# Chunk 4's columns on partitions without TensorE transposes

## The chip, the core and the metric

The kernel runs on one core of one Trainium2 chip. The metric is the device time of one execution in microseconds. A core has TensorE (PE, with its weight loads as PEld), VectorE (DVE), ScalarE (ACT), GpSimd (POOL) and SyncE (SP). SP does no arithmetic here; it issues most of the transfers, ACT and POOL issue the rest.

## What is computed

There are 2048 positions of 448 channels. With `xn` the layer norm of q over the channels, the result is a sum of three:

```python
xn = (q - mean) / sqrt(var + 1e-5)
ks = sum(k_pad[t:t+S] * shift_k[:, 3-t] for t in range(4))   # short causal filter
kv = ks * v
y  = causal_conv(kv, ssm_k) + kv * ssm_D                     # 2048 taps per channel, by FFT
out = q + xn * y + mish(xn @ w1 + b1) @ w2                   # w1 448x1792, w2 1792x448
```

The result is to have the accuracy of float32, so every dense product is made of three products of parts (a high part, rounded to the fast float32 form, and the low remainder).

## The kernel before

The positions are cut into 8 chunks of 256 (two halves `jj` of 128 each), and the 1792 hidden features into 7 pairs of 128. The program is a row of *slots*, two for each chunk and pair. An even slot holds the first dense layer of pair i (`g1_mm`, 22 matmuls, L509). An odd slot holds Mish of pair i (`mish`, L517, then the split into `ach` on ScalarE, L81, and `acl` on VectorE, L82) and the second dense layer of pair i−2 (`g2_mm`, 12 matmuls, L541 to L543). Slot 56 is the first of chunk 4, slot 70 the first of chunk 5.

All else is hung on the slots by hand: `at(slot, fn)` puts work ahead of a slot's dense layers, `after(slot, fn)` behind them. Every engine runs its own instructions strictly in the order in which they were written. `dv()` drips small VectorE jobs out of a list (`drip`) between larger ones.

The convolution runs beside the dense layers. In slots 6 to 32 the filter is transformed in 8 groups; in slots 24 to 59 (`KV_AT`, L27) 8 groups of k·v are. For group g, `taps` (L181) makes four shifted products on VectorE (L186, L189, L191, added up by L196, times v by L199). The product for the third shift is made on GpSimd by `taps_pool` (L176), released by a small VectorE memset (L178). Then `f1_mm` (L136, L143) multiplies the group by the constant `f1` on TensorE, `f1_fold` (L153) adds and subtracts the halves, and `f1_out` stores them to DRAM (`Dkv`). Group 6 goes to TensorE ahead of slot 55's dense layer, group 7 ahead of slot 59's. Later stages (L232, L254, L271 in slots 66 to 89, L328 from slot 98) read the stores back and invert the transform; `gate` (L332) multiplies by the normalised q, which `q_load` (L317) loads once more.

Each chunk has to stand with its channels on partitions (`XH`, `XL`) before its first slot. There are two ways:

- Chunks below `NT` (0 to 4): `ln_stats` (L424) takes the mean and variance on VectorE (L403, L406, L409), the power −1/2 on GpSimd (L412) and normalises on GpSimd (L416, L420). TensorE transposes each half with the identity (`transposes`, L461, four to a half), and the result in PSUM is split into `XH` on ScalarE (L473) and `XL` on VectorE (L471).
- Chunks from `NT` on (5 to 7): a second copy of q is loaded that is already turned (`xT_load`, L431). The statistics are taken as above, but GpSimd stores them to DRAM (`nt_store`, L439); SP loads them again as a row that is repeated over all partitions, once for each half (`nt_row`, L442, into `idr`), and VectorE subtracts and multiplies (`nt_norm`, L448, two instructions to a half). ScalarE casts `XH` (L455) and VectorE subtracts `XL` (L456).

`NT_AT` (L33) gives the slots of these steps relative to a base `b`, which is the first slot of chunk c less 14, plus 1 where c is `NT` itself:

```python
NT_AT = {"q": -5, "x": -1, "stats": -2, "flush": 0, "row": (4, 8), "norm": (7, 10), "split": (8, 11)}
b = 2 * NP * (c - 1) + (1 if c == NT else 0)
```

The buffer `idr` (128 x 256) holds the identity and `f1` at first, and the statistics' rows later. The second row load overwrites the first row, so it waits for `nt_norm` of the first half.

Of the kernel before, what the change touches and what calls it, by code (L numbers as in the profile page):

```python
# [7 lines left out]
F32 = mybir.dt.float32  # L8
# [8 lines left out]
NF = F // 128  # L17
NP = NF // 2
CH = 256
# [9 lines left out]
OCT_AT = (66, 3)  # L29
I2_AT = {98: (6, 7), 102: (0, 1), 106: (2, 3), 110: (4, 5)}  # L30
LATE = 2
NT = 5
NT_AT = {"q": -5, "x": -1, "stats": -2, "flush": 0, "row": (4, 8), "norm": (7, 10), "split": (8, 11)}  # L33
NT_LAST = dict(NT_AT, row=(4, 5), norm=(4, 7), split=(6, 8))
WARM_N = (448, 448, 448)
# [4 lines left out]
def tile_kernel(ctx: ExitStack, tc, q, qT, k, v, sk, hT, sD, w10, w1, w2, c_fib, c_g, c_gi, c_i2, out):  # L40
    nc = tc.nc
    V = nc.vector

    def pool(name, bufs=1, stack=ctx, **kw):
        return stack.enter_context(tc.tile_pool(name=name, bufs=bufs, **kw))

    cp = pool("consts")
# [13 lines left out]
    E = dp.tile([NJ * 4, 64, D], F32, name="E")  # L61
    MR = {c: dp.tile([2, CH], F32, name="MR") for c in range(NT, NCHUNK)}

    idr = cp.tile([128, CH], F32, name="idr")
    ident, f1 = idr[:, 0:128], idr[:, 128:192]
    mhalf = cp.tile([128, 2], F32, name="mhalf")
    b1t = cp.tile([128, NF], F32, name="b1t")
    mv = cp.tile([128, NJ, 2], F32, name="mv")
# [3 lines left out]
    def rs(c):  # L72
        return rstd[:, 2 * c:2 * c + 2] if c < NT else mv[:, 2 * c:2 * c + 2, 1]

# [34 lines left out]
    def at(slot, fn, *args):  # L109
        plan.setdefault(int(slot), []).append((fn, args))  # L110
# [13 lines left out]
    def kr():  # L124
        return sp1.tile([128, 4, CH], F32, name="kr", bufs=4)
# [266 lines left out]
    def xn_tile():  # L392
        return mp.tile([128, 4, CH], F32, name="xn", bufs=1)

    def ln_parts(c):
        st = mp.tile([128, 2, 6], F32, name="bst", bufs=2)
        ve = mp.tile([128, 2], F32, name="ve", bufs=2)
        if c < NT:
            XN[c] = xn = xn_tile().rearrange("p a b -> p (a b)").rearrange("p (j d) -> p j d", j=2)
# [75 lines left out]
    def ln_T(c, jj):  # L475
        if jj == 0:
            dv(len(drip))
            x_tiles(c)
        p = pg()
        transposes(c, jj, p)  # L480
        for lo in range(2):
            x_split(c, jj, p, lo)
# [73 lines left out]
    def mlp_slot(s):  # L556
# [3 lines left out]
        if half == 0:  # L560
            if i < n:
                c, p = pairs[i]
                if c + 1 < NT:
                    if p == 0:
# [8 lines left out]
        else:  # L573
            if i < n:
                c, p = pairs[i]
                if p == NP - 2 and c + 1 < NT:
                    ln_T(c + 1, 0)
# [72 lines left out]
    ts = sorted(I2_AT)  # L650
# [5 lines left out]
            at(t + 2 + m, gate_out, c)  # L656
            after(t - 4 + m if n else t - 3 + m, fold, c)
    for c in range(NCHUNK - LATE):
        at(ts[0] - (3 if c < 2 else 4), q_load, c, nc.sync if c < 2 else nc.gpsimd)

    for c in range(NT, NCHUNK):
        at_ = NT_LAST if c == NCHUNK - 1 else NT_AT
# [26 lines left out]
    nc.gpsimd.tensor_tensor(ve1, one, mhalf, op=ALU.pow)  # L689
    ln_load(0)  # L690
    RW["1", 0] = kr().rearrange("p a b -> p (a b)").rearrange("p (n a b) -> p n a b", n=2, a=4)
    nc.scalar.dma_start(idr[:, 0:192 + NF], c_fib)
    nc.gpsimd.tensor_copy(b1t, idr[:, 192:192 + NF])
    nc.sync.dma_start(RW["1", 0][:, 0], w10[:, 0])
    h_load(H_HEAD)
    nc.sync.dma_start(RW["1", 0][:, 1], w10[:, 1])
# [124 lines left out]
```

## Time and profile before

| what | value |
|---|---|
| median of 3 runs (lowest, highest) | 361.26 us (361.06, 361.45) |
| the profiled execution | 361.1 us, its span 359.3 us |
| granted TensorE clock, mean of the span | 1.0 |
| bytes moved | 81.69 MB, 227 GB/s |
| transposes L461 | 40 of 128x128, mean 278 ns |
| normalising on GpSimd L416 | 8, mean 2719 ns |
| normalising on VectorE L448 | 12, mean 690 ns |

In a row of the profile, `L448 DVE ... xn<-xn,idr` is an instruction of source line 448 on VectorE that writes tile `xn` from `xn` and `idr`; sizes are partitions by elements. In a timeline, the first number is the start in us from the span's start, the second the length. A bracket names how long the engine stood idle before the instruction and what ended that. A row of a table by windows gives the window, then busy time of PE, PEld, DVE, ACT and POOL, the granted TensorE clock, the share of the transfer engines and GB/s. A row of transfers gives queue, count, size and median time from issue to landing.

### The profile page before, as it was taken

Reading aid. Unit: us, or ns where it says so; the run is one execution under the profiler, and the core shown is the slowest. Engines: PE = TensorE matmul, PEld = TensorE weight load, DVE = VectorE, ACT = ScalarE, POOL = GpSimd, SP = SyncE. Lnnn points to the kernel's source line nnn. Section 1 sums busy time; section 2 is a strip of 40 time slices with the busy share of each in tenths; the row PEclk is TensorE's granted clock in tenths of the full one; section 3 lists DMA queues with packets and bytes.
Section 4 is the critical chain, followed back from the end, with each engine's and each line's share of the span. In section 5 each row is a group of like instructions: output and inputs, shape, how many; then the busy total and the mean of one; then the engine's idle time right before and its main releaser. Section 6 shows DMA issues by size and latency. Waiting matters only on the chain.

```text
span 359.3 us, 7451 instructions
## 1 busy us (share of the span) xinstructions
PE 354.0 (99%) x3108; PEld 291.0 (81%) x3108; DVE 266.1 (74%) x367; ACT 153.3 (43%) x263; POOL 82.3 (23%) x82
## 2 busy tenths in 40 slices
PE   8999999999999999999999999999999999999995
PEld 2988888888888989889997758766775699889885
DVE  5999748999998888798537847756963933997741
ACT  4967552344332343252333353455445443225450
POOL 2035002931028222704000030011031115112120
PEclk9999999999999999999999999999999999999999
DMA  7999969758686439533898578999895396969555
GB/s 249 355 370 322 418 246 241 221 157 268 153 259 202 93 122 276 132 94 81 243 284 289 201 182 292 234 278 309 282 267 126 80 287 231 407 263 274 100 73 132
DMA packets 29891, 81.69 MB, mean 227 GB/s; under 512 B 2977, under 2 KB 15138, under 8 KB 29858
## 3 DMA queue, kind: packets, MB, share of 16 engines
q1 hardware_dynamic: 21266, 47.16, 38.8%
q0 software_dynamic: 4704, 22.03, 22.5%
q10 hardware_dynamic: 3888, 12.03, 13.0%
q8 instruction: 24, 0.39, 0.4%
q14 instruction: 9, 0.07, 0.1%
HBM read 52.77 MB, written 28.45 MB: 226 GB/s over the span
## 4 chain that ended last, share of the span: by engine, by line
PE 56%; DVE 2%; issue 0%
PE pg L509 12%; PE pg L541 7%; PE pg L543 7%; PE pg L542 7%; PE pq L509 5%; PE pp L509 3%; PE pp L232 3%; PE pr L232 3%; PE pp L271 2%; PE pq L232 2%; PE pr L509 1%; PE pr L271 1%; PE pq L328 1%; PE pr L328 1%; DVE x L196 1%; PE pq L143 0%
## 5 line engine op out<-in xcount | busy, mean ns | idle before, releaser
L541 PE MATMUL pg<-w2h,ach 128*128 128x448 f32 x224 | 82.5, 368 | 0.0
L543 PE MATMUL pg<-w2h,acl 128*128 128x448 f32 x224 | 81.4, 363 | 0.0
L542 PE MATMUL pg<-w2l,ach 128*128 128x448 f32 x224 | 81.2, 363 | 0.0
L517 ACT ACTIVATE a<-pg,b1t 128x256 f32<-128x256 f32 x86 | 36.2, 472 | 87.2 <-PE pg L509 73.4
L509 PE MATMUL pg<-XH,w1h 128*128 128x256 f32 x344 | 69.1, 284 | 0.2 <-DVE XL L471 0.2
L82 DVE TENSOR_TENSOR acl<-a,ach 128x512 fp32r<-128x512 f32 x56 | 38.6, 690 | 35.9 <-ACT ach L81 35.7
L509 PEld LDWEIGHTS pg<-XH,w1h 128*128 128x128 f32 x344 | 53.8, 188 | 10.6 <-issue 8.6
L509 PE MATMUL pg<-XL,w1h 128*128 128x256 f32 x344 | 55.3, 277 | 0.0
L541 PEld LDWEIGHTS pg<-w2h,ach 128*128 128x128 f32 x224 | 41.9, 187 | 10.8 <-issue 7.2
L509 PEld LDWEIGHTS pg<-XL,w1h 128*128 128x128 f32 x344 | 46.5, 188 | 0.0
L542 PEld LDWEIGHTS pg<-w2l,ach 128*128 128x128 f32 x224 | 42.1, 188 | 2.4
L543 PEld LDWEIGHTS pg<-w2h,acl 128*128 128x128 f32 x224 | 42.0, 188 | 2.4
L509 PE MATMUL pg<-XH,w1l 128*128 128x256 f32 x258 | 43.7, 278 | 0.0
L153 DVE TENSOR_TENSOR st<-pq,st 128x896 f32<-128x896 f32 x32 | 34.8, 1088 | 3.7 <-ACT st L149 3.0
L509 PEld LDWEIGHTS pg<-XH,w1l 128*128 128x128 f32 x258 | 36.0, 188 | 0.0
L81 ACT CAST ach<-a 128x512 fp32r<-128x512 f32 x56 | 34.8, 622 | 1.7
L179 POOL TENSOR_TENSOR x<-kr,skb 128x896 f32<-128x896 f32 x8 | 17.0, 2127 | 75.5 <-DVE x L178 54.0
L196 DVE TENSOR_TENSOR x<-x 128x896 f32<-128x896 f32 x24 | 26.3, 1096 | 2.7 <-POOL x L179 2.2
L282 POOL DMA_DIRECT2D E<-qe x14 | 8.7, 628 | 63.7 <-ACT qe L279 63.6
L416 POOL TENSOR_SCALAR xn<-qt,mv,rstd 128x448 f32<-128x448 f32 x8 | 21.8, 2719 | 0.4
L149 ACT COPY st<-pr 128x896 f32<-128x896 f32 x16 | 14.5, 908 | 13.2 <-PE pr L143 12.6
L517 ACT ACTIVATE a<-pq,b1t 128x256 f32<-128x256 f32 x14 | 5.9, 471 | 26.7 <-PE pq L509 26.7
(137 smaller groups left out, 529.8 us busy)
## 6 DMA issues: line engine op xcount, KB each, us to landing
Dkv<-st ACTq DMA_DIRECT2D x16, 448.0 KB, 6.3
ah<-Dh SPq DMA_DIRECT2D x8, 896.0 KB, 7.7
av<-Dkv SPq DMA_DIRECT2D x8, 896.0 KB, 8.3
e<-E POOLq DMA_DIRECT2D x8, 896.0 KB, 8.5
E<-qe POOLq DMA_DIRECT2D x14, 448.0 KB, 5.9
kr<-in_k_dram SPq DMA_DIRECT2D x10, 448.0 KB, 6.4
Dh<-st ACTq DMA_DIRECT2D x10, 448.0 KB, 5.8
x<-in_hT_dram SPq DMA_DIRECT2D x8, 448.0 KB, 6.3
```

The source lines that it names most:

```text
L81: nc.scalar.copy(h, raw)
L82: V.tensor_sub(l, raw, h)
L153: f(st[:, n], e, st[:, 1])
L179: nc.gpsimd.tensor_mul(o, KR[g - u // 2], skb[:, u:u + 1].to_broadcast([128, 2, D]))
L196: V.tensor_add(KV[g], KV[g], o)
L232: nc.tensor.matmul(p[32 * t:32 * t + 32, r, :D], g[rs, t, c], a[rs, t], start=True, stop=True, tile_position=(64 * r, 32 * t))
L416: eng.tensor_scalar(xn[:, jj, :D], Q[c][:, jj], mv[:, j, 0:1], rs(c)[:, jj:jj + 1], op0=ALU.subtract, op1=ALU.mult)
L509: nc.tensor.matmul(ps[n], l, r, start=all(m[0] != n for m in seq[:n_]), stop=all(m[0] != n for m in seq[n_ + 1:]))
L517: nc.scalar.activation(a[:, n], ps[n], AF.Mish, bias=b1t[:, 2 * p + n:2 * p + n + 1])
L541: nc.tensor.matmul(ps, ah[:, n, cs], w2h[:, f], start=f == 0, stop=False)
L542: nc.tensor.matmul(ps, ah[:, n, cs], w2l[:, f], start=False, stop=False)
L543: nc.tensor.matmul(ps, al[:, n, cs], w2h[:, f], start=False, stop=f == NF - 1)
```

## The change

Chunk 4 moves from the first way to the second (`NT` 5 becomes 4). Its base is slot 43, so its statistics are at slot 41, its rows are loaded at slots 47 and 51, and its halves are normalised behind slots 50 and 53. The extra 1 goes from chunk 5 to chunk 4: chunk 5's base is 56 and no longer 57, and all its steps come one slot earlier. The constants move to a buffer `con`, in which `f1` stands ahead of the row buffer and is no longer overwritten. The q of chunks 0 and 1 for the gate is loaded on GpSimd's queue at slot 94, no longer on SP's at slot 95.

```diff
-NT = 5
+NT = 4
...
-    idr = cp.tile([128, CH], F32, name="idr")
-    ident, f1 = idr[:, 0:128], idr[:, 128:192]
+    con = cp.tile([128, 64 + CH], F32, name="con")
+    f1, ident, idr = con[:, 0:64], con[:, 64:192], con[:, 64:]
...
     for c in range(NCHUNK - LATE):
-        at(ts[0] - (3 if c < 2 else 4), q_load, c, nc.sync if c < 2 else nc.gpsimd)
+        at(ts[0] - 4, q_load, c, nc.gpsimd)
...
-    nc.scalar.dma_start(idr[:, 0:192 + NF], c_fib)
-    nc.gpsimd.tensor_copy(b1t, idr[:, 192:192 + NF])
+    nc.scalar.dma_start(con[:, 0:192 + NF], c_fib)
+    nc.gpsimd.tensor_copy(b1t, con[:, 192:192 + NF])
...
-    const["c_fib"] = np.concatenate([const.pop("c_id"), const.pop("c_f1"), a["B_b1"].reshape(NF, 128).T], axis=1)
+    const["c_fib"] = np.concatenate([const.pop("c_f1"), const.pop("c_id"), a["B_b1"].reshape(NF, 128).T], axis=1)
```

On GpSimd, around slots 48 to 60. Before, the last rows of chunk 4's normalising, then the taps of groups 6 and 7, then chunk 5's statistics and their store:

```order
L416 TENSOR_SCALAR xn<-qt,mv,rstd 128x448
L420 COPY xn<-xn 128x64
L179 TENSOR_TENSOR x<-kr,skb 128x896 x2
L412 TENSOR_TENSOR mv<-ve,mhalf 128x2
L439 DMA MR<-mv 128x2x2
```

After, chunk 4's statistics and store, the taps of groups 5 and 6, chunk 5's statistics and store, and then the tap of group 7:

```order
L412 TENSOR_TENSOR mv<-ve,mhalf 128x2
L439 DMA MR<-mv 128x2x2
L179 TENSOR_TENSOR x<-kr,skb 128x896 x2
L412 TENSOR_TENSOR mv<-ve,mhalf 128x2
L439 DMA MR<-mv 128x2x2
L179 TENSOR_TENSOR x<-kr,skb 128x896
```

The normalising is gone, and the power and the store of chunk 5 now stand ahead of group 7's tap.

On SP, slots 47 to 60. Before, from the k load of group 6 on: an output, v of group 6, k of group 7, q of chunk 5, v of group 7, the turned q of chunk 5:

```order
L169 DMA kr<-in_k_dram 128x896
L554 DMA out_dram<-qt 128x896
L173 DMA x<-in_v_dram 128x896
L169 DMA kr<-in_k_dram 128x896
L387 DMA qt<-in_q_dram 128x896
L173 DMA x<-in_v_dram 128x896
L431 DMA xn<-in_qT_dram 128x1024
```

After, from the same k load on, with chunk 4's two row loads:

```order
L169 DMA kr<-in_k_dram 128x896
L442 DMA con<-MR 128x256
L554 DMA out_dram<-qt 128x896
L173 DMA x<-in_v_dram 128x896
L442 DMA con<-MR 128x256
L387 DMA qt<-in_q_dram 128x896
L169 DMA kr<-in_k_dram 128x896
L173 DMA x<-in_v_dram 128x896
L431 DMA xn<-in_qT_dram 128x1024
```

The k and v of group 7 and the q of chunk 5 now stand behind the second row load.

On VectorE, from group 7's first tap (L186) to the end of group 7 (L199). Before, with `XL` of chunk 4 from PSUM:

```order
L186 TENSOR_TENSOR x<-kr,skb 128x896
L471 TENSOR_TENSOR XL<-pg_1825,XH 128x4x128
L189 TENSOR_TENSOR x<-kr,skb 128x448
L191 TENSOR_TENSOR x<-kr,skb 128x448
L196 TENSOR_TENSOR x<-x 128x896
L82 TENSOR_TENSOR acl<-a,ach 128x512
L403 BN_STATS bst<-qt 128x6
L178 MEMSET x 1x1
L153 TENSOR_TENSOR st<-pq,st 128x896
L403 BN_STATS bst<-qt 128x6
L153 TENSOR_TENSOR st<-pq,st 128x896
L406 BN_AGGR mv<-bst 128x2 x2
```

After, from the row behind L186 on:

```order
L448 TENSOR_TENSOR xn<-xn,con 128x4x128 x2
L189 TENSOR_TENSOR x<-kr,skb 128x448
L403 BN_STATS bst<-qt 128x6
L191 TENSOR_TENSOR x<-kr,skb 128x448
L403 BN_STATS bst<-qt 128x6
L196 TENSOR_TENSOR x<-x 128x896
L406 BN_AGGR mv<-bst 128x2
L456 TENSOR_TENSOR XL<-xn,XH 128x4x128
L406 BN_AGGR mv<-bst 128x2
L82 TENSOR_TENSOR acl<-a,ach 128x512
L409 TENSOR_SCALAR ve<-mv 128x2
L178 MEMSET x 1x1
```

The second pair of L448 stands between L186 and `XL`. Chunk 5's statistics are through, `ve` included, ahead of group 7's memset (L178), which the two L153 and the L196 that takes GpSimd's tap follow; before, they ran between and behind these.

## The prediction

> **What bounds the kernel now.** First the busy shares, then what TensorE waited for.
>
> ```profile
> PE 354.0 (99%) x3108; PEld 291.0 (81%) x3108; DVE 266.1 (74%) x367; ACT 153.3 (43%) x263; POOL 82.3 (23%) x82
> ...
> PE pg L685 <- DVE wz L681: 1.0, 1, 1.0
> ...
> PE pg L509 <- DVE XL L471: 0.2, 1, 0.2
> ```
>
> TensorE hardly rests: one stop at the start, and 0.2 us in the middle. So time taken off TensorE is worth its full length, and any other engine that makes TensorE wait costs its full length too. The one wait in the middle stands beside chunk 4's transposes. The timeline of TensorE there (start, length, what):
>
> ```profile
> 149.95 0.51 PE L509 MATMUL pg<-XH,w1h 128*128 128x256 f32 x3
> ...
> 152.46 0.60 PE L461 MATMUL pg<-idr,xn 128*128 128x128 f32 x4
> ...
> 156.12 0.62 PE L509 MATMUL pg<-XH,w1h 128*128 128x256 f32 x3 [0.20 <-DVE XL L471]
> ...
> 158.90 0.59 PE L143 MATMUL pq<-x,idr 32*64 32x448 f32 x2
> ...
> 162.36 0.52 PE L509 MATMUL pg<-XH,w1h 128*128 128x256 f32 x3
> ...
> 167.28 0.51 PE L509 MATMUL pg<-XH,w1h 128*128 128x256 f32 x3
> ...
> 169.88 0.59 PE L143 MATMUL pq<-x,idr 32*64 32x448 f32 x2
> ```
>
> The L509 rows open slots 52, 54, 56 and 58; the L143 rows are the products of k·v groups 6 (slot 55) and 7 (slot 59). Their operands come from VectorE, so VectorE's own timeline must be read against 158.90 and 169.88:
>
> ```profile
> 147.32 1.09 DVE L153 TENSOR_TENSOR st<-pq,st 128x896 f32<-128x896 f32 x1
> 150.44 1.09 DVE L196 TENSOR_TENSOR x<-x 128x896 f32<-128x896 f32 x1 [2.03 <-POOL x L179]
> ...
> 156.58 1.09 DVE L186 TENSOR_TENSOR x<-kr,skb 128x896 f32<-128x896 f32 x1
> ...
> 161.71 0.06 DVE L178 MEMSET x<- 1x1 f32 x1
> ...
> 164.37 1.06 DVE L196 TENSOR_TENSOR x<-x 128x896 f32<-128x896 f32 x1
> 165.34 0.17 DVE L409 TENSOR_SCALAR ve<-mv 128x2 f32<-128x2 f32 x1
> ...
> 167.73 1.09 DVE L199 TENSOR_TENSOR x<-x 128x896 f32<-128x896 f32 x1
> ...
> 172.31 2.22 DVE L153 TENSOR_TENSOR st<-pq,st 128x896 f32<-128x896 f32 x2
> ...
> 183.19 1.41 DVE L448 TENSOR_TENSOR xn<-xn,idr 128x512 f32<-128x512 f32 x2
> ```
>
> From 150.44 to 168.82 (167.73 + 1.09, the end of group 7) VectorE has no wait that the timeline names: 18.38 us of work in a row. It is done 1.06 us before TensorE asks at 169.88. That 1.06 us is the room the change has to live in.
>
> **What the transposes are worth.** An undisturbed pair of slots is 167.28 − 162.36 = 4.92. With the transposes, slots 52 and 53 and the second set take 156.12 − 149.95 = 6.17, so 1.25 comes back. The first layer behind them is slow as well: 158.90 − 156.12 = 2.78, against 169.88 − 167.28 = 2.60; another 0.18. Gain **1.43 us**: group 7 would be asked for at 168.45.
>
> **What VectorE gets.** Chunk 4's halves are now normalised on VectorE (four L448), and no longer on GpSimd. The split L456 replaces L471 one for one. GpSimd's rows:
>
> ```profile
> 145.23 2.79 POOL L416 TENSOR_SCALAR xn<-qt,mv,rstd 128x448 f32<-128x448 f32 x1
> ...
> 148.27 2.13 POOL L179 TENSOR_TENSOR x<-kr,skb 128x896 f32<-128x896 f32 x1
> 161.90 2.13 POOL L179 TENSOR_TENSOR x<-kr,skb 128x896 f32<-128x896 f32 x1 [11.50 <-issue]
> 165.59 1.02 POOL L412 TENSOR_TENSOR mv<-ve,mhalf 128x2 f32<-128x2 f32 x1 [1.56 <-DVE ve L409]
> 166.90 0.83 POOL L439 DMA_DIRECT2D MR<-mv  x1 [0.29 <-POOL mv L412]
> ```
>
> First a gain. The tap of group 6 (L179 at 148.27) stood behind the old normalising and made VectorE wait 2.03. Without L416 it starts 0.19 behind its memset, as the other one does (161.71, 161.90). That memset stands just ahead of the pair of L153 whose second half is at 147.32, one 1.09 earlier, so at 146.2; the tap ends near 146.4 + 2.13 = 148.54, and VectorE goes on at 148.58 and not at 150.44: −1.86.
>
> Then the cost of L448: two pairs of 1.41, each overlapping its neighbour by 0.08, 2.66. Group 7 would be ready at 168.82 − 1.86 + 2.66 = **169.62**. That alone is 1.2 later than 168.45: most of the gain is gone before any wait.
>
> **A detour on GpSimd.** Chunk 5's statistics move a slot earlier. In the order above, GpSimd's power (L412) and its store (L439) now stand ahead of group 7's tap (L179), where before they stood behind it. Before, that tap ran at 161.90 and was done at 164.03, in time for L196 at 164.37. Now it starts when ve, power and store are through: 167.73 − 165.34 = 2.39 after ve begins, is done 2.13 later and lets L196 start at about ve + 4.6. In that time VectorE has only the two L153, 2.22 (the row at 172.31). VectorE waits about 2.25; group 7 is ready at **171.9**.
>
> **A transfer that becomes late.** SP issues its transfers in program order. Its rows, one k load before and the three issues that follow a row load later on, and the landing times of all k loads:
>
> ```profile
> 137.82 1.07 SPq L169 DMA_DIRECT2D kr<-in_k_dram  x1
> ...
> 184.62 0.33 SPq L442 DMA_DIRECT2D idr<-MR  x1
> 185.00 0.43 SPq L387 DMA_DIRECT2D qt<-in_q_dram  x1
> 185.48 0.43 SPq L223 DMA_DIRECT2D gi<-in_c_gi_dram  x1
> ...
> DMA to landing us min/median/max: 5.3/6.4/12.6
> ...
> 148.68 1.24 ACTq L164 DMA_DIRECT2D Dkv<-st  x2
> ...
> 150.00:160.00 10.00, 9.80 (x82) 8.52 (x81) 9.46 (x13) 3.49 (x8) 0.41 (x1) 1.00 0.54 141
> ```
>
> Group 7's k was issued at 137.82 and used at 156.58 (L186). Now it stands behind the second row load of chunk 4, and that one waits until VectorE has read the first row (the first pair of L448). The pair starts when L196 is through, 148.58 + 1.09 − 0.08 = 149.59, and ends at 151.00. Then come row, q and k, as at 184.62, 185.00 and 185.48: k is issued at 151.86. L186 now wants it at 156.58 − 1.86 + 1.33 = 156.05. By the least landing of a k load, 5.3, it is there at 157.2 (wait 1.1); by the median 6.4 at 158.3 (wait 2.2). I take 2.2, because a row and a q lie ahead of it in its queue and ScalarE's two stores (148.68 before) now go out behind the cast XH at about 151.6 and share the engines. The upper end is 2.9: the 12.6 belongs to stages with the transfer engines full, here their share is 0.54. The lower end is 0.
>
> The Trainium skill, "DMA: Bandwidth & Descriptors", section "Anatomy of one DMA", gives 2.0 us plus bytes over 436 GB/s for one transfer, an estimate of 3.1 us for these 448 KB. By that k would be there at 155.0 and the wait would be nothing. The k loads of this trace took 5.3 and more, on another kind of queue than the page's fit, so I do not follow it.
>
> **The sum.** Group 7 is ready at 171.9 + 2.2 = 174.1, and TensorE starts it at about 174.15 and not at 169.88: **+4.3 us**, the 1.43 already in it. (On its way TensorE stops twice: in slot 56 for the low part XL of chunk 4, and again at slot 59. XL's last half comes behind L186, an L448 pair, four half-size operations of 0.6 and L196, 1.09 + 1.41 + 2.4 + 1.09, less overlaps of 0.08, from 158.3 on: near 164.5, against 161.7 where TensorE would want it. So the first stop is some 2.8 and the second 5.7 − 2.8, about 2.9.) Behind slot 59 TensorE has no idle time to take it back. Nothing there comes closer relative to it: chunk 5's normalising has a slot more, and the stores of group 7 and the loads behind them follow the product as before.
>
> **Edits at nothing.** f1 apart from the row buffer: it adds no instruction; it lets chunk 4's rows land while f1 is still read. The two loads of q leave SP and stand behind four loads of E on GpSimd's queue:
>
> ```profile
> 302.24 1.63 POOL L319 DMA_DIRECT2D q<-in_q_dram  x3
> ...
> 321.98 1.26 DVE L339 SCALAR_TENSOR_TENSOR q<-q,mv,pq 128x448 f32<-128x448 f32 x2
> ...
> 323.16 1.09 DVE L310 TENSOR_TENSOR ex<-e 128x896 f32<-128x896 f32 x1
> ...
> 310.22 1.49 POOL L304 DMA_DIRECT2D e<-E  x2 [5.82 <-PE pq L328]
> ...
> e<-E POOLq DMA_DIRECT2D x8, 896.0 KB, 8.5
> ...
> q<-in_q_dram POOLq DMA_DIRECT2D x3, 448.0 KB, 10.6
> ```
>
> The first q lands near 302.2 + 10.6 = 312.8 and is used at 321.98: 9 us of cover. What comes behind in the queue is two transfers later, some 3 us (an estimate from 448 KB every 1.5); the next load of E, issued at 310.22, landed near 318.7 (8.5 later) and would land near 321.7; it is used at 323.16. If that cover went, VectorE would lose a microsecond in a stage where TensorE waits for none of it. Zero.
>
> The profiled execution took 361.1 with a span of 359.3; the median of the runs is 361.26. So 361.26 + 4.3 = **365.5**.
>
> **Rivals.**
> 1. k lands in time. For it speak the v loads of the same size, which land faster:
>
> ```profile
> x<-in_v_dram SPq DMA_DIRECT2D x8, 448.0 KB, 3.9
> ```
>
>    Against it: the row, the q and the stores beside it. Only the detour on GpSimd is left: 171.9 + 0.06 − 169.88 = +2.1, 363.4. Chance 0.19.
> 2. TensorE's clock falls in the long stop. At the end of the program the clock falls late:
>
> ```profile
> 355.00:356.00 1.00, 0.60 (x3) 0.22 (x2) 0.42 (x2) 0.00 (x0) 0.00 (x0) 1.00 0.07 23
> ...
> 359.00:360.00 1.00, 0.00 (x0) 0.00 (x0) 0.00 (x0) 0.00 (x0) 0.00 (x0) 0.67 0.00 0
> ```
>
>    The last matmul ends at 355.6 and the clock is halved at about 359.3, so 3.7 us of rest were needed; my stops are 2.8 and 2.9. If one is enough, and the slow stretch lasts as long as the rest that sets it off (3.7, an estimate), half of that is lost: +1.85, 367.4. Chance 0.08. The Trainium skill, "TensorE: Matmul & The Clock Gate", section "Why this matters for your kernels", says that gaps over about 3 us send the array back to half rate; by that the long stop is on the edge, and the trace's 3.7 puts it below.
> 3. Neither detour nor k counts (if VectorE's order gave other work to fill both): 169.62, 1.2 behind 168.45, nets −0.2: 361.1. Chance 0.07.
> 4. The other side: VectorE's added work is hidden, because it has more room than one profile shows. TensorE then keeps all of 1.43: 359.8. It decides at group 7 being ready by 169.1 (later than that, under 0.72 us, which is 0.2%, is left). For it: VectorE's share of the span is only 74%, so it rests somewhere. Against it: in the 18.38 us that count it does not, and its rests behind slot 59 are of no use. Chance 0.10.
>
> **How the numbers follow.** The forecast has 0.56, and its own range, from a k wait of 1.1 to 2.9, is 364.4 to 366.2. The range given goes down to rival 1 (with 0.5 for errors in the durations) and up to rival 2: 362.9 to 367.4; left out are rivals 3 and 4, 0.17. 0.2% is 0.7 us, about what a measurement of this kernel can tell from none. Faster 0.10, same 0.07, slower 0.83.
>
> **What would show it.** Right: no L461 between 150 and 158; VectorE's L186 of group 7 with a wait for kr from memory; L196 with a wait for GpSimd's L179 of over 2 us, and L412 and L439 ahead of that L179; TensorE idle before the L509 of slot 56 (for XL) and before L143 of slot 59, 5 to 6 us in all; the time behind slot 60 unchanged. Wrong: L199 of group 7 ends before 169; TensorE idle under 1.5 us in 150 to 175; or new idle time on TensorE behind 290, where I see none.

## The result and the profile after

The changed kernel takes **366.12 us** (median of 4 runs, 365.48 to 367.01), the kernel before beside it 361.23. The ratio is 1.0137, with a 95% interval of 1.0125 to 1.0150: slower by 4.9 us. The forecast was 365.5 in a range of 362.9 to 367.4.

The profiled execution is the longest of the four, 0.9 above the median: 367.01 us, span 365.2, against 361.1 and 359.3 before. The busy shares and TensorE's waits in its middle:

```profile
PE 356.1 (98%) x3100; PEld 292.4 (80%) x3100; DVE 268.6 (74%) x371; ACT 153.5 (42%) x263; POOL 79.0 (22%) x81
...
PE pg L509 <- DVE XL L456: 2.0, 1, 2.0
PE pg L509 <- ACT XH L455: 1.9, 1, 1.9
```

The eight transposes are gone (3108 matmuls before, 3100 now). TensorE now stops twice in its middle. Its timeline (the openings of slots 52, 54 and 56, the low parts of slot 56, the opening of slot 58, the product of group 7):

```profile
150.13 0.52 PE L509 MATMUL pg<-XH,w1h 128*128 128x256 f32 x3
...
155.04 0.51 PE L509 MATMUL pg<-XH,w1h 128*128 128x256 f32 x3
...
163.19 0.62 PE L509 MATMUL pg<-XH,w1h 128*128 128x256 f32 x3 [1.93 <-ACT XH L455]
...
166.33 1.22 PE L509 MATMUL pg<-XL,w1h 128*128 128x256 f32 x4 [2.05 <-DVE XL L456]
...
175.96 0.59 PE L143 MATMUL pq<-x,con 32*64 32x448 f32 x2
```

Slots 52 and 53 take 155.04 − 150.13 = 4.91, where they took 6.17: that gain is there. But the product of group 7 starts at 175.96 and not at 169.88. That is 6.1 us later, and the span is 5.9 longer, so only 0.2 is given back behind it. VectorE, with what it waited for:

```profile
148.59 1.09 DVE L196 TENSOR_TENSOR x<-x 128x896 f32<-128x896 f32 x1
...
160.06 1.09 DVE L186 TENSOR_TENSOR x<-kr,skb 128x896 f32<-128x896 f32 x1 [3.92 <-DMA kr<-in_k_dram]
161.07 1.41 DVE L448 TENSOR_TENSOR xn<-xn,con 128x512 f32<-128x512 f32 x2
...
171.06 1.09 DVE L196 TENSOR_TENSOR x<-x 128x896 f32<-128x896 f32 x1 [1.91 <-POOL x L179]
...
174.38 1.09 DVE L199 TENSOR_TENSOR x<-x 128x896 f32<-128x896 f32 x1
```

Both predicted waits stand where they were put. The first is for k, whose issue and landing (SP's timeline, then the row of transfers) are:

```profile
151.03 0.32 SPq L442 DMA_DIRECT2D con<-MR  x1
151.45 0.39 SPq L387 DMA_DIRECT2D qt<-in_q_dram  x1
151.89 0.51 SPq L169 DMA_DIRECT2D kr<-in_k_dram  x1
...
kr<-in_k_dram SPq DMA_DIRECT2D x1, 448.0 KB, 8.1
```

The second is for GpSimd, which now runs power, store and tap in that order:

```profile
167.10 0.72 POOL L412 TENSOR_TENSOR mv<-ve,mhalf 128x2 f32<-128x2 f32 x1 [18.54 <-DVE x L178]
168.11 0.77 POOL L439 DMA_DIRECT2D MR<-mv  x1 [0.29 <-POOL mv L412]
168.91 2.12 POOL L179 TENSOR_TENSOR x<-kr,skb 128x896 f32<-128x896 f32 x1
```

One thing had a chance of only 0.08 in the forecast. The windows show TensorE's granted clock (the seventh column, behind the busy times) falling to half in the second stop and staying there; first in steps of 5 us, then in steps of half a microsecond:

```profile
160.00:165.00 5.00, 2.35 (x14) 1.72 (x12) 4.91 (x8) 2.45 (x5) 0.00 (x0) 1.00 0.04 16
165.00:170.00 5.00, 3.67 (x16) 3.67 (x17) 4.11 (x9) 0.40 (x2) 2.58 (x3) 0.54 0.34 109
170.00:175.00 5.00, 5.00 (x27) 4.66 (x27) 3.87 (x5) 1.39 (x3) 1.03 (x1) 0.78 0.58 126
...
165.00:165.50 0.50, 0.00 (x0) 0.00 (x0) 0.50 (x1) 0.33 (x1) 0.00 (x0) 0.90 0.07 16
165.50:166.00 0.50, 0.00 (x0) 0.00 (x0) 0.50 (x3) 0.00 (x0) 0.00 (x0) 0.50 0.00 0
...
172.00:172.50 0.50, 0.50 (x4) 0.48 (x3) 0.50 (x2) 0.00 (x0) 0.00 (x0) 0.78 0.92 201
```

The clock is at 0.50 from 165.4 to 172.2, for 6.8 us. At that clock TensorE reached slot 59 only at 175.96, 0.49 after VectorE had group 7 ready (174.38 + 1.09 = 175.47). So there is no stop at slot 59.

### The profile page after: what moved, and what is told of

Read it like the earlier page. It is cut to its first block, busy times and chain, and to the rows that moved or that the text cites. A ratio compares the mean times of both kernels' runs of the same rounds, so it can differ in the third digit from the quotient of the medians.

```text
span 365.2 us, 7439 instructions
## 1 busy us (share of the span) xinstructions
PE 356.1 (98%) x3100; PEld 292.4 (80%) x3100; DVE 268.6 (74%) x371; ACT 153.5 (42%) x263; POOL 79.0 (22%) x81
## 4 chain that ended last, share of the span: by engine, by line
PE 78%; issue 6%; DMA 6%; DVE 5%; POOL 3%; ACT 1%; SPq 0%; ACTq 0%; POOLq 0%
PE pg L509 22%; PE pg L541 11%; PE pg L543 10%; PE pg L542 10%; PE pq L509 5%; PE pp L509 3%; DMA Dh<-st 3%; PE pp L232 3%; PE pr L232 3%; PE pq L143 2%; DMA kr<-in_k_dram 2%; PE pp L271 2%; PE pq L232 2%; PE pr L509 1%; PE pr L271 1%
## 5 line engine op out<-in xcount | busy, mean ns | idle before, releaser
L509 PE MATMUL pg<-XL,w1h 128*128 128x256 f32 x344 | 56.2, 280 | 2.0 <-DVE XL L456 2.0
L153 DVE TENSOR_TENSOR st<-pq,st 128x896 f32<-128x896 f32 x32 | 34.8, 1089 | 6.0 <-ACT st L149 5.3
L196 DVE TENSOR_TENSOR x<-x 128x896 f32<-128x896 f32 x24 | 26.3, 1098 | 2.7 <-POOL x L179 2.1
L412 POOL TENSOR_TENSOR mv<-ve,mhalf 128x2 f32<-128x2 f32 x4 | 3.6, 910 | 71.6 <-DVE ve L409 53.0
L416 POOL TENSOR_SCALAR xn<-qt,mv,rstd 128x448 f32<-128x448 f32 x6 | 17.8, 2971 | 0.3
```

Of the source, the lines that this page charges most:

```text
L153: f(st[:, n], e, st[:, 1])
L196: V.tensor_add(KV[g], KV[g], o)
L416: eng.tensor_scalar(xn[:, jj, :D], Q[c][:, jj], mv[:, j, 0:1], rs(c)[:, jj:jj + 1], op0=ALU.subtract, op1=ALU.mult)
L509: nc.tensor.matmul(ps[n], l, r, start=all(m[0] != n for m in seq[:n_]), stop=all(m[0] != n for m in seq[n_ + 1:]))
```

## The experiments

### Which wait costs what

**e1: k of group 7 one slot earlier**, ahead of the second row load.

```diff
-        at(t - d - (3 if g > 1 else 2), k_load, g)
+        at(t - d - (4 if g == 7 else 3 if g > 1 else 2), k_load, g)
```

> The changed kernel with the k load of group 7 one slot earlier, ahead of chunk 4's second row load. My theory: the wait of VectorE's L186 for kr (3.92 us in the changed kernel) goes, L186 starts near 156.05, only the detour over GpSimd is left, and group 7 is ready near 171.9: 363.4 us. Rival (the late k only fills a rest that VectorE would have anyway, for GpSimd or for another transfer): 366.1, no change against the changed kernel.

**e2: chunk 5's statistics and store one slot later**, where they were before.

```diff
-        at(b + at_["stats"], nt_stats, c)
-        at(b + at_["flush"], lambda: dv(len(drip)))
+        at(b + at_["stats"] + (c == NT + 1), nt_stats, c)
+        at(b + at_["flush"] + (c == NT + 1), lambda: dv(len(drip)))
```

> The changed kernel with chunk 5's statistics and their store one slot later, where they were before, so that GpSimd's tap of group 7 stands ahead of the power and the store again. My theory: the wait of L196 for GpSimd (1.91 us) goes, the wait for kr (3.92) stays; the first-layer stop in slot 56 stays too, so the gain is at most 1.9 and rather 1.1 to 1.9: 364.2 to 365.0 us. Rival (VectorE only moves the wait, since the statistics now run between the taps and the product): 366.1.

**e3: both edits.**

> The changed kernel with both: k of group 7 one slot earlier and chunk 5's statistics one slot later. My theory: both waits go, what VectorE gets in L448 stays, group 7 is ready at 169.6, some 1.2 us after TensorE would ask for it without transposes: 361.1 us, the same as before the change, within 0.5. Rival A (the normalising on VectorE costs nothing once the waits are gone): 359.8. Rival B (a further cause that I have not seen holds part of the 4.9 us): 362 or more.

| kernel | median us | ratio to before (95%) |
|---|---|---|
| e1 | 363.19 | 1.0052 (1.0034 to 1.0069) |
| e2 | 364.21 | 1.0081 (1.0068 to 1.0094) |
| e3 | 360.26 | 0.9974 (0.9963 to 0.9984) |

The kernel before took 361.25 beside them. Of e1, VectorE's L196 and the product of group 7, then of e2 L186, then of e3 the same product:

```profile
166.78 1.09 DVE L196 TENSOR_TENSOR x<-x 128x896 f32<-128x896 f32 x1 [1.93 <-POOL x L179]
...
171.25 0.59 PE L143 MATMUL pq<-x,con 32*64 32x448 f32 x2 [2.25 <-DVE x L199]
```

```profile
159.63 1.09 DVE L186 TENSOR_TENSOR x<-kr,skb 128x896 f32<-128x896 f32 x1 [3.25 <-DMA kr<-in_k_dram]
```

```profile
169.05 0.59 PE L143 MATMUL pq<-x,con 32*64 32x448 f32 x2 [0.74 <-DVE x L199]
```

Each edit takes away its own wait and leaves the other: in e1 VectorE waits 1.93 for GpSimd and not for k, in e2 3.25 for k and not for GpSimd. So the rivals of e1 and e2 (the wait only moves) fall. The waits add up: with k already in time, GpSimd's is worth 362.36 − 360.26 = 2.1 (362.36 is the mean of e1's four runs at a clock of 1.0, below); with GpSimd in time, k's is worth 364.21 − 360.26 = 3.95. e1 came within 0.2 of my 363.4, e2 at the lower end of my 364.2 to 365.0. e3 came out between my 361.1 and rival A's 359.8: 0.74 of a stop is left at slot 59, where I had worked out 1.2.

### What the transposes and the normalising are worth

**e5: the kernel before without chunk 4's transposes.**

```diff
-        p = pg()
-        transposes(c, jj, p)
+        if c == 4:
+            p = XN[c][:, jj]
+        else:
+            p = pg()
+            transposes(c, jj, p)
```

> The kernel before with chunk 4's eight transposes left out: its XH and XL are split from xn as it lies, so chunk 4's part of the result is of other numbers. All else stands as before. My theory: TensorE gets 1.43 us shorter (1.25 in slots 52 and 53, 0.18 behind), and group 7, ready 1.06 us before it was asked for, then holds it up by 0.4 at most: 359.8 to 360.3 us. Rival (the transposes lie beside other waits and cost nothing): 361.2.

**e4: e2, with chunk 4's rows and halves earlier.**

```diff
+NT_FIRST = dict(NT_AT, row=(4, 5), norm=(4, 7), split=(5, 8))
...
-        at_ = NT_LAST if c == NCHUNK - 1 else NT_AT
+        at_ = NT_LAST if c == NCHUNK - 1 else NT_FIRST if c == NT else NT_AT
```

> The changed kernel with chunk 5's statistics one slot later, and chunk 4's two row loads and its normalising some three slots earlier, so that the first pair of L448 falls into a rest of VectorE near 141 to 143 and the second row, q and k are issued near 143. My theory: k is there in time, GpSimd is ahead, and one pair of L448 lies in idle time: group 7 is ready near 168.3, as TensorE asks for it, and the gain of the transposes is kept: 359.8 us, faster than both kernels. Rival (other work of VectorE is pushed back by the earlier pairs, group 6 for one): 361 or more.

e5: 359.61, ratio 0.9957 (0.9944 to 0.9969), 1.5 us, just under the 359.8 that I expected at the least. The transposes of chunk 4 cost what their slots showed. e4: 359.45, ratio 0.9952 (0.9938 to 0.9966). Of the kernels that leave nothing out it has the lowest median, 1.8 us under before and 6.7 under the changed one. The changed kernel's VectorE has a rest ahead of slot 50:

```profile
143.40 0.69 DVE L82 TENSOR_TENSOR acl<-a,ach 128x512 fp32r<-128x512 f32 x1 [2.04 <-ACT ach L81]
```

In e4 VectorE's rows (one line of the source is new, so L449 is L448, and so on) and the two products of slots 55 and 59:

```profile
139.88 1.41 DVE L449 TENSOR_TENSOR xn<-xn,con 128x512 f32<-128x512 f32 x2
...
143.37 0.69 DVE L83 TENSOR_TENSOR acl<-a,ach 128x512 fp32r<-128x512 f32 x1 [0.47 <-ACT ach L82]
...
156.06 1.08 DVE L187 TENSOR_TENSOR x<-kr,skb 128x896 f32<-128x896 f32 x1
...
166.44 1.09 DVE L200 TENSOR_TENSOR x<-x 128x896 f32<-128x896 f32 x1
...
157.25 0.59 PE L144 MATMUL pq<-x,con 32*64 32x448 f32 x2
...
168.32 0.59 PE L144 MATMUL pq<-x,con 32*64 32x448 f32 x2
```

The first pair now lies at 139.88 and fills the rest: 0.47 of the 2.04 is left. k is issued at 142.68 and costs no wait. Group 7 is ready at 167.53, 0.8 before TensorE takes it without a stop at 168.32. So the 0.8 between e3 and e4 is what the place of the pairs is worth: in e3 TensorE stops 0.74 at slot 59, in e4, with one pair moved into a rest, not at all.

**e6: the changed kernel with NT 5**, so only `con` and the two loads of q are left of the change.

> The changed kernel with chunk 4 prepared in the old way (NT 5): of the change only f1 apart from the row buffer and the two loads of q on GpSimd's queue are left. My theory: 361.2 us, no change against the kernel before, within 0.3. Rival (the q loads behind E hold the gate or the next E): 361.7 or more, with new waits behind 300 us.

361.20, ratio 0.9998 (0.9989 to 1.0007): nothing, as the prediction had it for these edits.

**e7: e4 with chunk 3 in the new way too.** The table NT_FIRST and the extra slot of the base then hold for chunks 3 and 4.

```diff
-NT = 4
+NT = 3
...
-        b = 2 * NP * (c - 1) + (1 if c == NT else 0)
+        b = 2 * NP * (c - 1) + (1 if c <= 4 else 0)
```

> The kernel of e4 with chunk 3 prepared in the new way as well (its rows and halves 14 slots ahead of chunk 4's). If the gain of the transposes holds wherever VectorE has the room, another 1.4 us goes: 358.0 us. VectorE rests 1.8 us between 115 and 120 us, and group 4 is ready 2.6 us before TensorE asks for it, so I expect it to have the room. Rival (VectorE is late for a product in slots 34 to 44): 359.5 or more, with a wait of TensorE for L200.

361.52, ratio 1.0004 (0.9994 to 1.0015): 2.1 us lost against e4, and my forecast of 358.0 missed. GpSimd in e7, and VectorE behind it:

```profile
88.97 1.08 POOL L413 TENSOR_TENSOR mv<-ve,mhalf 128x2 f32<-128x2 f32 x1 [13.44 <-DVE ve L410]
90.35 0.83 POOL L440 DMA_DIRECT2D MR<-mv  x1 [0.29 <-POOL mv L413]
91.21 2.13 POOL L180 TENSOR_TENSOR x<-kr,skb 128x896 f32<-128x896 f32 x1
...
93.37 1.09 DVE L197 TENSOR_TENSOR x<-x 128x896 f32<-128x896 f32 x1 [1.75 <-POOL x L180]
```

It is the detour of the changed kernel once more, now at group 1: power and store ahead of a tap.

**e10: e7 with chunk 3's statistics one slot later.**

```diff
-        at(b + at_["stats"] + (c == 5), nt_stats, c)
-        at(b + at_["flush"] + (c == 5), lambda: dv(len(drip)))
+        at(b + at_["stats"] + (c in (3, 5)), nt_stats, c)
+        at(b + at_["flush"] + (c in (3, 5)), lambda: dv(len(drip)))
```

> The kernel of e7 (chunks 3 and 4 in the new way) with chunk 3's statistics and their store one slot later, behind GpSimd's tap of group 1. e7 showed VectorE waiting 1.75 us for that tap behind the power and the store. My theory: that wait goes, and with it the two stops of TensorE for qt (1.5 us): 358.0 to 359.5 us, below e4 if VectorE has room for two more pairs. Rival (VectorE is too full there in any case): 360.5 or more.

360.73, ratio 0.9983 (0.9973 to 0.9993). The wait for GpSimd is gone and 0.8 us with it, but my 358.0 to 359.5 missed, and e4 stays 1.3 faster. First, chunk 3's transposes were worth less than chunk 4's: from the product of slot 39 to the next first layer e4 takes 117.92 − 113.72 = 4.20 and e10 117.63 − 114.18 = 3.45, a gain of 0.75 and not 1.4. Second, TensorE stops at the end of a chunk, where VectorE comes too late to empty the second layer's sums:

```profile
137.10 0.45 PE L542 MATMUL pg<-w2h,ach 128*128 128x448 f32 x1 [0.82 <-DVE qt L549]
```

So the rival (VectorE is too full there) holds for this 0.8. With the gain of 0.75 e10 would take some 358.7 and takes 2.0 more; the rest of that lies where the profile names no wait of TensorE, and stays open.

### Why k took 8.1 us

**e11: ScalarE's stores of group 5 one slot later.**

```diff
-        at(t + (3 if g < NO - 1 else 2), f1_out, Dkv, g, "kv")
+        at(t + (4 if g == 5 else 3 if g < NO - 1 else 2), f1_out, Dkv, g, "kv")
```

> The changed kernel with ScalarE's two stores of group 5 (issued at 151.05, while k of group 7 is on its way) one slot later. If these stores make k land in 8.1 us and not in 6.4, it now lands in 6 to 6.5 us, VectorE's wait for kr goes from 3.9 to about 2.2, and the time from 366.1 to 364.5 or so. Rival (the transfers ahead of k on its own queue make it late, as the next run tests): 366.1, landing 8.

**e12: q of chunk 5 behind k on SP's queue.**

```diff
-        at(b + at_["q"], ln_load, c)
+        at(b + at_["q"] + (c == NT + 1), ln_load, c)
```

> The changed kernel with the 448 KB load of chunk 5's q behind k of group 7 on SP's queue and no longer ahead of it. If the q ahead makes k late, k is issued some 0.4 us earlier and lands in 6 us or less: the wait for kr goes from 3.9 to 1.5 or so, the time to 364.0. Rival (the stores on ScalarE's queue are the cause): 365.7, only the 0.4 us of the earlier issue. Q is wanted near 160 and should land before.

The landing and the wait in e11, then the wait in e12:

```profile
kr<-in_k_dram SPq DMA_DIRECT2D x1, 448.0 KB, 6.1
...
157.76 1.09 DVE L186 TENSOR_TENSOR x<-kr,skb 128x896 f32<-128x896 f32 x1 [1.96 <-DMA kr<-in_k_dram]
```

```profile
152.23 0.38 SPq L169 DMA_DIRECT2D kr<-in_k_dram  x1
...
158.00 1.09 DVE L186 TENSOR_TENSOR x<-kr,skb 128x896 f32<-128x896 f32 x1 [1.09 <-DMA kr<-in_k_dram]
```

Without the stores beside it k lands in 6.1, without the q ahead of it in at most 158.00 − 152.23 = 5.8. With both it took 8.1 in the changed kernel, 7.5 in e2 and 7.2 in e9. So taking either away wins 1.1 to 2.3 us and brings k back under the median of 6.4, and both rivals held in part. The two shares do not simply add: both taken off would leave 3.8 to 4.7 us, and no such load of k in any run here landed in less than 4.9. Nor does it take the stores: in e4, where v and q of 448 KB each are issued just ahead of k (141.73, 142.21) and no store of ScalarE's between 134.00 and 151.05, k landed as late as in the changed kernel, but it was issued nine us earlier:

```profile
kr<-in_k_dram SPq DMA_DIRECT2D x1, 448.0 KB, 8.1
```

So what counts is how much goes out just ahead of k and beside it; how the transfers share the engines is not shown. e12 takes 364.06 (1.0075, 1.0053 to 1.0097), as expected, though k was issued no earlier than in the changed kernel (152.23), so that all it won is in the landing. e11 takes 366.07 (1.0111, 1.0084 to 1.0138), no less than the changed kernel although its wait is 2 us shorter; its runs say why: two at a mean clock of 1.0 took 364.2, four at 0.995 took 365.9 to 366.5.

### The clock

The windows of e11's profiled run, one of the four, show where the clock goes, in the seventh column (three of 5 us, two of half a microsecond, then the product of group 7):

```profile
165.00:170.00 5.00, 5.00 (x37) 4.85 (x37) 3.03 (x4) 1.46 (x3) 3.42 (x3) 1.00 0.69 182
170.00:175.00 5.00, 2.68 (x26) 1.08 (x24) 4.32 (x6) 1.46 (x3) 0.00 (x0) 0.81 0.88 216
175.00:180.00 5.00, 5.00 (x34) 4.75 (x29) 3.24 (x4) 0.91 (x1) 0.00 (x0) 0.85 0.48 148
...
173.00:173.50 0.50, 0.26 (x8) 0.26 (x16) 0.50 (x2) 0.00 (x0) 0.00 (x0) 0.59 0.48 66
176.50:177.00 0.50, 0.50 (x4) 0.46 (x4) 0.50 (x1) 0.00 (x0) 0.00 (x0) 1.00 0.54 196
...
173.24 1.01 PE L143 MATMUL pq<-x,con 32*64 32x448 f32 x2 [2.32 <-DVE x L199]
```

It holds at 1.0 into the stop of 2.32 at slot 59, falls to 0.50 at 173.1, some 2.2 us after the last matmul, and is back at 176.5: 3.4 us at half. e1 gave two groups as well: 362.21 to 362.57 at 1.0 (four runs, the profiled one with its stop of 2.25 among them), 363.80 to 364.28 at 0.995 (four).

**e8: e1 with 14 matmuls nobody reads ahead of group 7's product.**

```diff
         PS[key, g] = ps = [pc(1), pc(2)]
+        if (key, g) == ("kv", 7):
+            for _ in range(14):
+                nc.tensor.matmul(ps[0][:, 0, :CH], w1h[:, 0, 0:128], XS[4][0][:, 0], start=True, stop=True)
```

> The kernel of e1 with 14 matmuls of 128x256 more on TensorE, whose sums nobody reads, ahead of group 7's product, where TensorE stops for 2.25 us. 14 by 0.115 us are 1.6 us, so they fit in. e1 gave two groups of times, 362.2 to 362.6 with a mean clock of 1.0 and 363.8 to 364.3 with 0.995. My theory (the stop sets off a fall of the clock in some executions): with the filler the second group is gone, all runs near 362.4 with a clock above 0.998. Rival (the two groups have another cause, memory for one): both groups stay.

362.21 (1.0029, 1.0018 to 1.0041). TensorE at slot 59 (the new lines are L139 to L141, L146 is L143):

```profile
169.58 1.75 PE L141 MATMUL pq<-XH,w1h 128*128 128x256 f32 x14
171.98 0.59 PE L146 MATMUL pq<-x,con 32*64 32x448 f32 x2 [0.65 <-DVE x L202]
```

The upper group is gone: of six runs five took 361.99 to 362.32 and one (the profiled one) 363.03, all with a clock of 0.998 or more. TensorE does more work, and the median is a microsecond lower, though the intervals of the two ratios overlap. Six runs without a fall, against four of eight with one, could still be chance. The runs of all kernels together leave little room for it: of the 32 runs of the six kernels whose profile shows a stop in the middle of 1.3 or more (the changed one, e1, e2, e9, e11, e12) 17 have a mean clock of 0.995 or less; of the 112 runs of the others, the kernel before included, whose longest stop there is 0.82, none is below 0.997. So the fall goes with the stop; the rival, another cause of the two groups, falls.

**e9: the changed kernel with fillers**, 12 ahead of slot 56's first layer and 8, as in e8, ahead of group 7.

```diff
+        if i == 28:
+            for _ in range(12):
+                nc.tensor.matmul(ps[0], w1h[:, 0, 0:128], XS[3][0][:, 0], start=True, stop=True)
         if i == 0:
```

> The changed kernel with matmuls of 128x256 more whose sums nobody reads: 12 ahead of slot 56's first layer (1.4 us of the 1.93 us that TensorE stops there) and 8 ahead of group 7's product (0.9 us). My theory: the clock stays up (mean above 0.998 in all runs), but VectorE still has group 7 ready no earlier than in the changed kernel (175.47), which TensorE reached only 0.5 us late with the halved clock, so no more than 0.5 us is won: 365.6 us. Rival (the fall costs what it costs in the kernel of e1, 1.6 us): 364.5.

365.64 (1.0114, 1.0094 to 1.0133), 0.5 less than the changed kernel, as expected. Two of the four runs still show 0.995 (365.82 both), against my "all above 0.998": stops of 1.92 for XL and 1.33 at slot 59 are left. In the changed kernel the fall thus costs about half a microsecond, because VectorE is late anyway: the profile bounds it by the 0.49 of above, and the intervals of the two ratios (e9 and the changed kernel) overlap.

## Why the prediction held, step by step

- **Gain of the transposes, 1.43**: 1.5 (e5). Right for chunk 4; chunk 3's were worth half of it (e10).
- **Group 6's tap no longer behind the normalising**: VectorE goes on at 148.59, forecast 148.58. Right.
- **L448, +2.66, in a stretch without rest**: right as a mechanism; that the kernel then nets −0.2 was too dark. With both waits gone e3 nets −1.0, since the stop left at slot 59 is 0.74 and not 1.2, and some 0.3 of the difference lies ahead of slot 52 (149.66 in e3, 149.95 before; 150.13 in the changed kernel), where the profiled runs scatter by about that much.
- **Detour on GpSimd, 2.25**: the wait is 1.91 (my sign was over 2), its removal is worth 2.1. Right. L412 took 0.72, not the 1.02 of the old row.
- **Late k, 2.2 (0 to 2.9)**: issued at 151.89 against 151.86, but landed after 8.1 and not 6.4; the wait is 3.92, outside my bounds. This is the term that was mis-sized. I had named the q ahead and the stores beside it, and then taken the median of loads of which only one (issued at 78.30, with no landing on record) has both; my upper end of 2.9 came from no row. e11 and e12 show that either one taken away brings the landing to about 6. The 3.1 us that I had estimated from the Trainium skill ("DMA: Bandwidth & Descriptors", "Anatomy of one DMA") is further off still; no k load here was that quick (4.9 at the least, in e3).
- **Two stops of 2.8 and 2.9, at XL and at slot 59**: there were two, but both in slot 56 (1.93 and 2.05), 4.0 together and not 5 to 6; the halved clock took up the rest. I overlooked that XH waits for the second pair of L448 as well, so that slot 56 does not even begin:

```profile
162.52 0.62 ACT L455 CAST XH<-xn 128x512 fp32r<-128x512 f32 x1 [8.18 <-DVE xn L448]
```

- **f1 and the q loads at zero**: right (e6).
- **Rival 2, the clock**: I gave it 0.08, since it wanted a rest of 3.7 us. That condition came from one profile and was wrong: at the ends of the fourteen profiled runs the clock falls anywhere from 2.0 us (e3) to 5.3 us (e4) after the last matmul, and 3.7 is just where the kernel before happened to lie. The rival came in in part. Its price of 1.85 was good where TensorE sets the end: e1's groups are 1.65 apart, e11's 2.0, about half of the 3.4 us that e11's clock is down.
- **Rival 4, the gain kept**: not in this order of the work, but e4 shows that it was to be had.

That the sum came within 0.6 of the median is in part luck, since errors cancel. In the profiled run, 1.5 above the forecast, k cost 1.7 more, the clock came on top with some 0.5, and the normalising cost 0.8 less. No trace shows k's landing in the other three runs.

## What to carry to other kernels

Work taken off the busiest engine is worth only what the engine that takes it over has in rests, in that stage: the same four instructions cost 0.8 us in one place (e3) and nothing some three slots earlier (e4). Where engines run in program order, moving a small step also moves a short operation past a tap, or a load behind one that waits; here these two cost 2.1 and 3.95 us, more than the 1.5 that was to be won. Price a moved transfer by what will stand ahead of it in its queue and beside it on other queues, not by the median of its kind.

## What the chip showed that I had not expected

- TensorE's clock falls in stops well under 3.7 us: in the changed kernel in the second of two stops, of 1.93 and 2.05 with 1.1 us of matmuls between them (0.54 in the window 165 to 170), in e11 in one of 2.32 (with 2.06 some 7 us earlier), and in four runs of eight of e1, whose stop is 2.25. It was then at half for 3.4 us in e11 and for 6.8, twice as long, in the changed kernel. The Trainium skill ("TensorE: Matmul & The Clock Gate", "Why this matters for your kernels") speaks of gaps over about 3 us; these runs put it lower, and not at one sharp length. Its section "What's actually happening" says that the clock is set by how busy TensorE was in a free-running window of 3.4 us; where a stop lies in such a window could be what differs from run to run. The 3.4 and 6.8 us at half, and the ends of the programs, spread over 3.3 us (2.0 to 5.3), fit that; but no run here moves a stop on purpose to test it, and what decides it stays open.
- Matmuls whose result nobody reads can pay: e8's 14 fillers left no run in e1's slower group, 1.65 us above the other, and cost the faster group nothing that shows (medians of 362.21 and, in that group of e1, 362.32).
